# Bias of the spectral mix by a matmul that opens the accumulation, and the soft threshold as the minimum of y + lambda and relu(y - lambda), read out of PSUM

## Chip, cores and metric

One core of one Trainium2 chip runs the kernel. The metric is the device time of one execution in microseconds. Before the change it is 3775.99 us, the median of 3 runs (3766.45 to 3784.93).

## What is computed

The input x has 8 batches of 3072 rows of 256 features. Three stages follow each other:

```python
X = np.fft.rfft(x, axis=1)
Yr = Xr @ w_r - Xi @ w_i + b_r
Yi = Xr @ w_i + Xi @ w_r + b_i
lam = 0.01
Yr = np.sign(Yr) * np.maximum(np.abs(Yr) - lam, 0.0)
Yi = np.sign(Yi) * np.maximum(np.abs(Yi) - lam, 0.0)
y = np.fft.irfft(Y, n=x.shape[1], axis=1)
...
out[do_compute] = xc + gate_w * (relu(xc @ w1[e]) @ w2[e])
...
return elu(h @ w_in) @ w_out
```

The middle two lines, for the 24,576 rows of the first stage's result, are a mixture of 8 experts, of which each token takes the best one, if it takes any. The last is a dense layer with an ELU.

## The kernel before

The program has three phases, one after the other. The first does the transform along the sequence, the spectral mix and the routing of the tokens, the second the experts (a loop over tiles of 384 tokens), the third the dense layer. The change touches the first phase alone.

**The transform.** 3072 is split as 96 x 32. `forward` (L398 on) reads a batch in 8 pieces of 96 x 4 x 256 (tile `x`, for the first batch also `yv`), rounds each to float32r (`xa`), takes the rest (`xb`), multiplies with the constant `fh` and its rest `fl` on TensorE (L424, three matmuls in place of one of full precision), copies the result out of PSUM (`av`) and stores it to DRAM (`ta`). The constant `fwd` comes in 8 pieces through the tile `tr`, of which 3 live at a time; `tr` also stages the other constants, among them `w_r` and `w_i`, and later holds what the inverse transform reads.

**The middle.** `middle` takes a batch in 12 pieces p of two tiles each, and for every second batch a 13th of one tile for frequency 48: 100 pieces in all, 96 of them with two tiles. A piece is loaded (`t`), goes through the DFT of length 32 (L470, `ps<-mb,t`) and is rounded and split from PSUM (`xh` on ScalarE, `xl` on VectorE). Then comes the mix, 12 matmuls of 256 columns for each tile (L501), so 24 for a piece, into one PSUM bank `py`. Behind the mix stand three VectorE steps:

```python
nc.vector.tensor_tensor(v(y), self.tiles[py][:, :n, :], self.bias.to_broadcast([128, n, D]), op=ALU.add)
nc.vector.tensor_scalar(v(c), v(y), LAM, -LAM, op0=ALU.min, op1=ALU.max)
nc.vector.tensor_tensor(v(y), v(y), v(c), op=ALU.subtract)
```

The first (L510) adds the bias and frees the bank, the second (L517) clips to plus or minus lambda, the third (L522) takes the clipped part off. ScalarE rounds the result (`sh`), VectorE or GpSimd takes the rest (`sl`, L235), and three matmuls of 512 columns (L534, `ps<-sh,mph` and so on) start the inverse transform. The result is copied out (`cv`) and stored (`ct`).

**The inverse and the routing.** `inverse` reads `ct` in 8 pieces (`tr`), rounds and splits them (`th`, `tl`), multiplies with `inh` and `inl` (L576), turns the blocks (L589, `turn`), splits them again (`yth`, `ytl`) and computes the gate's logits (L634). `route` turns these into list positions: a chain of small VectorE steps that ends in `cnt` (L723), two small matmuls (L731, L732), `ix` (L743), and then GpSimd scatters the tokens to the experts' lists, 12 or 6 instructions for a chunk (L748). `Prep` splits the third phase's float64 weights on VectorE in the same stretch (L853 to L874).

**What sets the order.** All of the first phase is a list of steps in `Flow`. Each step has an engine (or several that can take it, with a cost for each), a due time, and the tiles that it reads and writes; of each tag, a fixed number of tiles lives at a time (7 PSUM banks `ps`, one `c`, two each of `y`, `sh`, `sl`). `Flow.order` builds the instruction order of every engine ahead of time with these costs: of the steps that could start first, the one that is due first. Roundings (`round`) go to ScalarE or VectorE, rests (`rest2`) to VectorE or GpSimd, whichever would end first by these costs. The costs are the numbers in the code, and a change in one moves steps on all engines. DMAs are issued from two queues: loads from the SyncE queue (SP), stores of `ta`, `ct` and the rows of the result from the ScalarE queue. Each queue and each engine runs in its order.

Of the kernel before, what the change touches and what calls it, by code (L numbers as in the profile page):

```python
# [11 lines left out]
F32 = mybir.dt.float32  # L12
F32R = mybir.dt.float32r
I32 = mybir.dt.int32
AF = mybir.ActivationFunctionType
ALU = mybir.AluOpType
AX = mybir.AxisListType

B, S, D = 8, 3072, 256
# [12 lines left out]
def shape_constants():  # L32
    # rows of a tile: real parts of frequencies 2 t and 2 t + 1, then imaginary parts; frequency 48 alone at the end
# [11 lines left out]
    for j in range(2):  # L45
# [11 lines left out]
    f = np.float32  # L57
    return {
# [4 lines left out]
        "tri": np.triu(np.ones((128, 128), f), 1),  # L63
    }


class Flow:
    """Steps of the engines in the order in which their inputs, buffers and engines come free.

    A step reads and writes tiles by key (tag, ...); of a tag, bufs[tag] tiles live at a time.  # L70
    Of the steps that could start, an engine takes the one that is due first.
    """
# [6 lines left out]
    def add(self, ways, due, r=(), w=(), since=0):  # L79
        """ways: (engine, cost, what to do) of each engine that can take the step."""  # L80
# [13 lines left out]
    def order(self):  # L94
        """The steps' actions in order of their start."""
# [57 lines left out]
class Phase1:  # L153
# [93 lines left out]

    def consts(self):
# [3 lines left out]
        wst = lambda: self.t(("tr", "w")).rearrange("p (h i) d -> p h (i d)", h=2)  # noqa: E731  # L252
# [3 lines left out]
        self.bias = cr.tile([128, 1, 256], F32, tag="bias", name="bias")  # L256
# [5 lines left out]
        for q in range(8):  # L262
# [6 lines left out]
            at = lambda v, s=s: v[:, s, :]  # noqa: E731  # L269
# [15 lines left out]
        def load_m():  # L285
            nc.sync.dma_start(mpf, c["mp"])
            for i, v in enumerate((self.b_r, self.b_i)):
                nc.sync.dma_start(
                    self.bias[64 * i : 64 * i + 64, 0, :], v.rearrange("(o d) -> o d", o=1).to_broadcast([64, 256])
                )  # L290

        add("DMA", 1350, -1.5, load_m, w=[("r", "mp")])
# [20 lines left out]
        trif = lambda: self.t(("tr", "tri"))[:, 0, 0:128]  # noqa: E731  # L313
        self.tri = cp.tile([128, 128], F32R, tag="tri", name="tri")
        zero = cp.tile([128, D // 128], F32, tag="zero", name="zero")
        pad = cp.tile([128, 98, 2], I32, tag="pad", name="pad")
# [5 lines left out]
        def small():  # L322
            nc.vector.memset(zero, 0.0)
            nc.vector.memset(pad[:, :, 0:1], 0)
# [68 lines left out]

    def at(self, b):
        """When the middle of batch b is due."""
        return 12 * b + (b + 1) // 2
# [943 lines left out]
```

## Time and profile before

| | |
|---|---|
| median of 3 runs | 3775.99 us (3766.45 to 3784.93) |
| span of the profiled execution, first to last instruction | 3687.1 us |
| median less the span | 88.9 us |
| first phase | about 0 to 885 us of the span |
| second phase | about 885 to 1535 us |
| third phase | about 1535 to 3687 us |
| busy share of the span | TensorE 96%, VectorE 66%, ScalarE 64%, GpSimd 18% |

The page lists the span of the profiled execution and not its own time; the time is set against the median of the runs, and the 88.9 us between the two lie around the span. The shares are means over three phases with different limits, so the first phase has to be read by itself, from the busy times of its stretches and from what its engines waited for. Line numbers are those of the kernel before. A matmul's row shows how long one takes from start to end; matmuls overlap, so what one costs in a row of them is the distance between starts.

### The profile page before, as it was taken

To read this page: it belongs to the slowest core of one execution; us is meant where nothing else is said; L and a number is where in the kernel's file an instruction comes from. 1 tells how busy PE (TensorE), PEld (TensorE's weight loads), DVE (VectorE), ACT (ScalarE), POOL (GpSimd) and SP (SyncE) were. 2 spreads that over 40 slices of the span, in tenths; PEclk is the share of its full clock that TensorE was granted. 3 is DMA by queue.
4 is the path that set the end of the run, shared out by engine and by line. 5 is a ranking of instruction groups with operands and counts; after the bars stand their busy time and mean duration, and the time that the engine had idled before them with its cause. 6 is when DMAs were issued, how large, how long until landed. Compare 5 with 4: busy or idle time off the path is not lost.

```text
span 3687.1 us, 60200 instructions
## 1 busy us (share of the span) xinstructions
PE 3546.0 (96%) x20256; PEld 3131.5 (85%) x20256; DVE 2425.7 (66%) x4475; ACT 2345.5 (64%) x4483; POOL 671.2 (18%) x742
## 2 busy tenths in 40 slices
PE   7998999996999999799999999999999999999999
PEld 7988888885999999688888888888888888888888
DVE  6988989995777777555555555555555555555555
ACT  5665656553556556466666666666666666666666
POOL 0153654445454445200000000000000000000000
PEclk8999999998999999899999999999999999999999
DMA  8876766664555555611111111111110111111100
GB/s 231 250 210 200 212 196 201 184 191 132 164 161 165 162 162 169 171 24 23 24 24 23 24 24 23 29 30 24 24 23 24 23 24 24 23 24 24 23 18 18
DMA packets 280331, 341.30 MB, mean 93 GB/s; under 512 B 129105, under 2 KB 225898, under 8 KB 280113
## 3 DMA queue, kind: packets, MB, share of 16 engines
q1 hardware_dynamic: 222240, 234.67, 23.1%
q10 hardware_dynamic: 41216, 76.56, 6.5%
q0 software_dynamic: 16656, 27.21, 2.5%
q8 instruction: 131, 2.15, 0.3%
q14 instruction: 88, 0.71, 0.1%
HBM read 214.02 MB, written 126.05 MB: 92 GB/s over the span
## 4 chain that ended last, share of the span: by engine, by line
PE 58%; DMA 0%; DVE 0%; SPq 0%; ACT 0%; issue 0%; DVEq 0%
PE ph L1198 29%; PE py L1229 19%; PE py L1232 10%; DMA x<-x 0%; SPq L1176 0%; DVE o L1239 0%; DVE xt L1185 0%; ACT xh L1187 0%; DVE xl L1188 0%; ACT o L1238 0%; DVEq L1185 0%
## 5 line engine op out<-in xcount | busy, mean ns | idle before, releaser
L1229 PE MATMUL py<-wo,gh 128*128 128x512 f32 x3072 | 1116.6, 397 | 0.0
L1198 PE MATMUL ph<-xh,wi 128*128 128x512 f32 x3072 | 1080.4, 392 | 20.2 <-ACT xh L1187 20.1
L1211 DVE SCALAR_TENSOR_TENSOR e<-m,ph 128x512 f32<-128x512 f32 x768 | 528.6, 688 | 843.1 <-ACT m L1210 843.1
L1232 PE MATMUL py<-wo,gl 128*128 128x256 f32 x3072 | 863.2, 281 | 0.0
L1209 ACT ACTIVATE m<-ph 128x512 f32<-128x512 f32 x768 | 456.6, 594 | 462.1 <-PE ph L1198 459.4
L1198 PEld LDWEIGHTS ph<-xh,wi 128*128 128x128 f32 x3072 | 577.6, 188 | 150.7 <-ACT xh L1187 21.2
L1229 PEld LDWEIGHTS py<-wo,gh 128*128 128x128 f32 x3072 | 577.3, 188 | 137.1
L1232 PEld LDWEIGHTS py<-wo,gl 128*128 128x128 f32 x3072 | 576.8, 188 | 32.4
L1198 PE MATMUL ph<-xl,wi 128*128 128x512 f32 x1536 | 603.3, 393 | 0.0
L1218 DVE TENSOR_TENSOR gl<-e,gh 128x512 fp32r<-128x512 f32 x768 | 526.4, 685 | 0.2 <-ACT gh L1217 0.2
L1210 ACT ACTIVATE m<-m 128x512 f32<-128x512 f32 x768 | 485.4, 632 | 24.6
L1217 ACT ACTIVATE gh<-e 128x512 fp32r<-128x512 f32 x768 | 472.8, 616 | 0.3 <-DVE e L1211 0.3
L1198 PEld LDWEIGHTS ph<-xl,wi 128*128 128x128 f32 x1536 | 289.8, 189 | 34.9 <-DVE xl L1188 0.9
L1053 PE MATMUL py<-w2x,hh 128*128 128x512 f32 x864 | 306.3, 395 | 0.0
L748 POOL DMA_INDIRECT lst<-pay,ix x192 | 228.4, 1190 | 118.5 <-DVE ix L743 53.8
L1056 PE MATMUL py<-w2x,hl 128*128 128x256 f32 x864 | 241.9, 280 | 0.0
L501 PE MATMUL ps<-wh,xh 128*128 128x256 f32 x784 | 228.2, 291 | 5.4 <-ACT av L228 3.6
L501 PE MATMUL ps<-wh,xl 128*128 128x256 f32 x784 | 225.2, 287 | 3.0 <-DVE xl L244 2.6
L501 PE MATMUL ps<-wl,xh 128*128 128x256 f32 x784 | 224.5, 286 | 0.0
L1042 ACT ACTIVATE hh<-ph 128x384 fp32r<-128x384 f32 x288 | 141.5, 491 | 89.1 <-ACT w2x L1017 58.1
L1040 PE MATMUL ph<-xh,w1h 128*128 128x384 f32 x576 | 193.3, 336 | 0.7 <-DVEq L1116 0.7
L1040 PE MATMUL ph<-xl,w1h 128*128 128x384 f32 x576 | 193.1, 335 | 0.0
(188 smaller groups left out, 5783.5 us busy)
## 6 DMA issues: line engine op xcount, KB each, us to landing
w1r<-in_moe_w_dram SPq DMA_DIRECT2D x37, 1024.0 KB
w2r<-in_moe_w_dram SPq DMA_DIRECT2D x37, 1024.0 KB
ta<-av ACTq DMA_DIRECT2D x64, 392.0 KB
tr<-ct SPq DMA_DIRECT2D x64, 392.0 KB
t<-ta SPq DMA_DIRECT2D x96, 256.0 KB
ct<-cv ACTq DMA_DIRECT2D x96, 256.0 KB
x<-yv ACTq DMA_DIRECT2D x64, 384.0 KB
x<-x SPq DMA_DIRECT2D x192, 128.0 KB
```

The source lines that it names most:

```text
L501: nc.tensor.matmul(o[:, t, :], a[:, 2 * t + h, at : at + 128], w[:, h, ws], start=k == 0, stop=k == 11)
L1040: nc.tensor.matmul(ph, w[:, h, fs], x[:, h, :], start=k == 0, stop=k == 5)
L1053: nc.tensor.matmul(py.rearrange("p a d -> p (a d)"), self.hh[:, f, js], self.w2x[:, f, :], start=f == 0, stop=False)
L1056: nc.tensor.matmul(py[:, 0, :], self.hl[:, f, js], self.w2x[:, f, 0:256], start=False, stop=f == nf - 1)
L1198: nc.tensor.matmul(ph, w[:, h, fs], x[:, h, :], start=k == 0, stop=k == 5)
L1209: nc.scalar.activation(m, ph, AF.Relu, scale=-1.0)
L1210: nc.scalar.activation(m, m, AF.Exp, scale=-1.0)
L1211: nc.vector.scalar_tensor_tensor(e, m, 1.0, ph, op0=ALU.subtract, op1=ALU.max)
L1217: nc.scalar.activation(gh, e, AF.Copy)
L1218: nc.vector.tensor_tensor(gl, e, gh.bitcast(F32), op=ALU.subtract)
L1229: nc.tensor.matmul(py.rearrange("p a d -> p (a d)"), gh[:, js], self.wo[:, f, :], start=f == 0, stop=False)
L1232: nc.tensor.matmul(py[:, 0, :], gl[:, js], self.wo[:, f, 0:256], start=False, stop=f == 15)
```

## The change

The bias leaves VectorE. A constant `sel` of 34 x 128 has ones in rows 0 and 32 for the first 64 output rows (real parts) and in rows 1 and 33 for the last 64 (imaginary parts). A tile `bias` of 34 x 256 holds the two bias vectors rounded to float32r in rows 0 and 1 and their rests in rows 32 and 33. One matmul of `sel` with `bias`, repeated for both tiles of a piece (512 columns), opens the accumulation of each mix; the 24 matmuls of the mix now only add, and one of them, the last, closes. The soft threshold becomes two steps: ScalarE writes c = relu(y - lambda) out of PSUM, and VectorE writes the minimum of y + lambda and c, y again out of PSUM. The loads of the two bias vectors, broadcast to 64 rows each, are replaced by a memset, a load of `sel`, four loads of one row each and the rounding; they are staged through a tile of the tag `tr`. The costs of the steps in the order's list are set anew with the steps.

```diff
+    sel = np.zeros((34, 128), f)
+    for i in range(2):
+        sel[[i, 32 + i], 64 * i : 64 * i + 64] = 1.0
...
-        self.bias = cr.tile([128, 1, 256], F32, tag="bias", name="bias")
+        self.sel, self.bias = (cr.tile([34, n], F32R, tag=t, name=t) for t, n in (("sel", 128), ("bias", 256)))
+        bsel = lambda: self.t(("tr", "b"))[:34, 1, :128]
+        braw = lambda: self.t(("tr", "b"))[:34, 0, :]
...
         def load_m():
             nc.sync.dma_start(mpf, c["mp"])
+
+        def load_b():
+            nc.sync.dma_start(bsel(), c["sel"])
             for i, v in enumerate((self.b_r, self.b_i)):
-                nc.sync.dma_start(
-                    self.bias[64 * i : 64 * i + 64, 0, :], v.rearrange("(o d) -> o d", o=1).to_broadcast([64, 256])
-                )
-
-        add("DMA", 1350, -1.5, load_m, w=[("r", "mp")])
+                for at in (i, 32 + i):
+                    nc.sync.dma_start(braw()[at : at + 1, :], v.rearrange("(o d) -> o d", o=1))
+
+        def bias_hi():
+            self.copy(self.sel, bsel())
+            self.copy(self.bias, braw())
+
+        add("DMA", 450, -1.5, load_m, w=[("r", "mp")])
+        add("DVE", 300, -3, lambda: nc.vector.memset(braw(), 0.0), w=[("tr", "b")])
+        add("DMA", 2250, -2.5, load_b, w=[("tr", "b")])
+        add("ACT", 600, -1, bias_hi, r=[("tr", "b")], w=[("r", "bhi")])
+        add(
+            "DVE", 350, -0.5, lambda: self.rest(self.bias[32:34, :], braw()[32:34, :], self.bias[32:34, :]),
+            r=[("tr", "b"), ("r", "bhi")], w=[("r", "bias")],
+        )
...
             def mix(xh=xh, xl=xl, py=py, n=n):
                 o, xh, xl = self.p(py, [128, 2, D]), self.t(xh), self.t(xl)
+                bias = self.bias.rearrange("p (o d) -> p o d", o=1).to_broadcast([34, n, D])
+                nc.tensor.matmul(o[:, :n, :], self.sel, bias, start=True, stop=False)
...
-                                    o[:, t, :], a[:, 2 * t + h, at : at + 128], w[:, h, ws], start=k == 0, stop=k == 11
+                                    o[:, t, :], a[:, 2 * t + h, at : at + 128], w[:, h, ws], start=False,
+                                    stop=k == 11 and t == n - 1,
...
-            add("PE", 2600 * f, d + 1, mix, r=[xh, xl, ("r", "wh"), ("r", "wl")], w=[py])
-
+            add("PE", 2830 * f, d + 1, mix, r=[xh, xl, ("r", "wh"), ("r", "wl"), ("r", "bias")], w=[py])
+
+            add(
+                "ACT", 480 * f, d + 1.5,
+                lambda c=c, py=py, n=n, v=v: nc.scalar.activation(
+                    v(c), self.tiles[py][:, :n, :], AF.Relu, bias=self.lam
+                ),
+                r=[py], w=[c],
+            )
             add(
                 "DVE", 600 * f, d + 1.5,
-                lambda y=y, py=py, n=n, v=v: nc.vector.tensor_tensor(
-                    v(y), self.tiles[py][:, :n, :], self.bias.to_broadcast([128, n, D]), op=ALU.add
+                lambda y=y, c=c, py=py, n=n, v=v: nc.vector.scalar_tensor_tensor(
+                    v(y), self.tiles[py][:, :n, :], LAM, v(c), op0=ALU.add, op1=ALU.min
                 ),
-                r=[py, ("r", "mp")], w=[y],
-            )
-            add(
-                "DVE", 335 * f, d + 1.5,
-                lambda y=y, c=c, v=v: nc.vector.tensor_scalar(v(c), v(y), LAM, -LAM, op0=ALU.min, op1=ALU.max),
-                r=[y], w=[c],
-            )
-            add(
-                "DVE", 600 * f, d + 1.5,
-                lambda y=y, c=c, v=v: nc.vector.tensor_tensor(v(y), v(y), v(c), op=ALU.subtract),
-                r=[c], w=[y],
+                r=[py, c], w=[y],
             )
```

Since `Flow.order` works with the new steps and costs, every engine's order moves. Of the steps that may go to either of two engines, VectorE takes 46 more roundings that ScalarE had (19 of `yth`, 9 `yv`, 7 `av`, 8 `xa`, 3 `th`) and one piece of `fh`; of the rests it takes 6 `tl` and 4 `xb` more from GpSimd and gives it 7 `sl`. TensorE has 100 matmuls more and VectorE 147 rows fewer.

**VectorE at the first pieces of the first batch's middle.** `wb`, `wa` and `wq` belong to the splitting of the third phase's weights, `inl` is a constant of the inverse. Before:

```order
L510 TENSOR_TENSOR y<-ps,bias 128x512
L244 TENSOR_TENSOR xl<-ps,xh 128x4x128
L517 TENSOR_SCALAR c<-y 128x512
L856 SCALAR_TENSOR_TENSOR wa<-bits,wa 128x512
L522 TENSOR_TENSOR y<-y,c 128x512
L510 TENSOR_TENSOR y<-ps,bias 128x512
L244 TENSOR_TENSOR inl<-tr,inh 98x384
L235 TENSOR_TENSOR sl<-y,sh 128x512
```

Now:

```order
L542 SCALAR_TENSOR_TENSOR y<-ps,c 128x512
L249 TENSOR_TENSOR xl<-ps,xh 128x4x128
L875 TENSOR_SCALAR wb<-bits 128x512
L240 TENSOR_TENSOR sl<-y,sh 128x512
L876 TENSOR_SCALAR wb<-wb 128x512
L877 TENSOR_SCALAR wa<-wb 128x512
L542 SCALAR_TENSOR_TENSOR y<-ps,c 128x512
```

Of a piece's three steps between mix and rounding one is left, and the rest `sl` follows three rows behind `y`, where it was seven rows behind the first of the three.

**ScalarE at the same place.** Before:

```order
L241 ACTIVATE xh<-xh 128x4x64
L241 ACTIVATE xl<-xl 128x4x64
L241 ACTIVATE inh<-tr 98x384
L241 ACTIVATE sh<-y 128x512
L241 ACTIVATE xh<-ps 128x4x128
```

Now:

```order
L535 ACTIVATE c<-ps,lam 128x512
L246 ACTIVATE xh<-ps 128x4x128
L246 ACTIVATE sh<-y 128x512
L246 ACTIVATE xh<-xh 128x4x64
L246 ACTIVATE xl<-xl 128x4x64
L535 ACTIVATE c<-ps,lam 128x512
```

The relu of each piece stands as one more ScalarE step ahead of the piece's rounding `sh`, with one or more steps of other pieces between them.

**The SP queue at the start.** Here the last pieces of the constant `fwd`, the bias and the mix's weights are loaded among the pieces of x. Before:

```order
L407 DMA yv<-in_x_dram 96x1024
L267 DMA tr<-in_fwd_dram 96x392 x3
L407 DMA yv<-in_x_dram 96x1024
L407 DMA x<-in_x_dram 96x1024
L275 DMA mb<-in_mb_dram 128x128
L279 DMA tr<-in_w_r_dram 128x2x256
L279 DMA tr<-in_w_i_dram 128x2x256
L286 DMA mpf<-in_mp_dram 128x128
L288 DMA bias<-in_b_r_dram 64x256
L288 DMA bias<-in_b_i_dram 64x256
L407 DMA x<-in_x_dram 96x1024 x6
```

Now:

```order
L274 DMA tr<-in_fwd_dram 96x392 x2
L429 DMA yv<-in_x_dram 96x1024
L429 DMA x<-in_x_dram 96x1024
L296 DMA tr<-in_sel_dram 34x128
L299 DMA tr<-in_b_r_dram 1x256 x2
L299 DMA tr<-in_b_i_dram 1x256 x2
L282 DMA mb<-in_mb_dram 128x128
L293 DMA mpf<-in_mp_dram 128x128
L429 DMA x<-in_x_dram 96x1024
L274 DMA tr<-in_fwd_dram 96x392
L429 DMA x<-in_x_dram 96x1024
L286 DMA tr<-in_w_r_dram 128x2x256
```

The bias takes five issues in place of two and stands ahead of the last piece of `fwd`, which now comes after the first piece of the second batch's x.

## Rows read from the trace of the kernel before

**Rows 1.** The page: span, and TensorE's busy tenths in 40 slices.
```profile
span 3687.1 us, 60200 instructions
...
PE   7998999996999999799999999999999999999999
```

**Rows 2.** Windows by stage: us; busy us (count) by engine; clock; DMA share; GB/s.
```profile
0.00:75.00 75.00, 52.31 (x308) 49.33 (x309) 43.69 (x96) 39.80 (x69) 6.92 (x19) 0.80 0.85 248
75.00:815.00 740.00, 683.32 (x5245) 649.54 (x5244) 661.26 (x1171) 451.33 (x873) 309.45 (x204) 0.97 0.69 203
815.00:885.00 70.00, 39.22 (x277) 33.98 (x275) 44.27 (x171) 26.15 (x49) 49.50 (x48) 0.79 0.55 165
...
1535.00:3687.10 2152.10, 2143.51 (x10752) 1808.54 (x10752) 1188.54 (x1920) 1453.87 (x2592) 0.00 (x0) 1.00 0.12 27
```

**Rows 3.** Windows of 100 us in the first phase, columns as in rows 2.
```profile
100.00:200.00 100.00, 96.78 (x771) 93.11 (x770) 88.58 (x141) 65.12 (x123) 13.59 (x7) 1.00 0.85 252
...
300.00:400.00 100.00, 87.62 (x627) 82.41 (x628) 84.75 (x148) 58.05 (x111) 50.11 (x34) 0.91 0.69 199
...
700.00:800.00 100.00, 97.66 (x777) 93.16 (x777) 92.71 (x181) 61.19 (x127) 39.07 (x34) 1.00 0.59 174
```

**Rows 4.** TensorE's waits, 75 to 815 us: total us, times, longest us.
```profile
PE ps L534 <- DVE sl L235: 10.9, 13, 1.8
PE ps L534 <- POOL sl L235: 9.4, 6, 2.6
PE pl L634 <- DVE ytl L244: 7.8, 4, 4.2
PE ps L731 <- DVE cnt L723: 7.6, 4, 3.2
PE ps L534 <- ACT sh L241: 6.4, 7, 1.7
PE ps L424 <- DVE xl L244: 4.0, 1, 4.0
...
PE ps L501 <- DVE xl L244: 2.6, 2, 1.6
```

**Rows 5.** VectorE's groups, first phase: busy us, mean ns, idle us before them.
```profile
L522 DVE TENSOR_TENSOR y<-y,c 128x512 f32<-128x512 f32 x96 | 66.6, 694 | 0.4
...
L510 DVE TENSOR_TENSOR y<-ps,bias 128x512 f32<-128x512 f32 x96 | 65.6, 683 | 3.8 <-PE ps L501 3.6
...
L517 DVE TENSOR_SCALAR c<-y 128x512 f32<-128x512 f32 x96 | 46.3, 482 | 0.6
```

**Rows 6.** Groups of operations like those that the change adds or moves.
```profile
L1211 DVE SCALAR_TENSOR_TENSOR e<-m,ph 128x512 f32<-128x512 f32 x768 | 528.6, 688 | 843.1 <-ACT m L1210 843.1
...
L228 ACT ACTIVATE cv<-ps 128x512 f32<-128x512 f32 x83 | 49.2, 593 | 42.0 <-PE ps L534 34.3 <-DMA ct<-cv 4.0 <-DMA bits<-in_moe_w_out_dram 1.6
...
L229 DVE COPY cv<-ps 128x512 f32<-128x512 f32 x13 | 8.9, 683 | 1.2 <-PE ps L534 1.2
...
L235 DVE TENSOR_TENSOR tl<-tr,th 98x1024 fp32r<-98x1024 f32 x45 | 58.7, 1304 | 7.1 <-ACT th L228 6.2 <-DMA bits<-in_moe_w_in_dram 0.7
```

**Rows 7.** TensorE's timeline, three matmuls of 512 columns in a row: start, us.
```profile
761.03 0.40 PE L534 MATMUL ps<-sl,mph 128*128 128x512 f32 x1
761.26 0.39 PE L534 MATMUL ps<-sh,mpl 128*128 128x512 f32 x1
761.50 0.28 PE L501 MATMUL ps<-wh,xh 128*128 128x256 f32 x1
```

**Rows 8.** TensorE's longest kind of single wait in the first 75 us.
```profile
PE ps L424 <- ACT xa L228: 8.6, 3, 6.2
```

**Rows 9.** GpSimd's timeline at the first phase's end: first and last scatter, first gather.
```profile
817.58 0.99 POOL L748 DMA_INDIRECT lst<-pay,ix  x1 [10.09 <-DVE lt L649]
...
880.44 0.98 POOL L748 DMA_INDIRECT lst<-pay,ix  x1 [0.30 <-issue]
885.11 1.04 POOL L974 DMA_INDIRECT rn<-x,pn  x1 [3.69 <-issue]
```

More of the change, by code (lines that the diff above doesn't have):

```diff
@@ L63, in shape_constants @@
         "tri": np.triu(np.ones((128, 128), f), 1),
+        "sel": sel,
     }
@@ L315, in consts @@
         zero = cp.tile([128, D // 128], F32, tag="zero", name="zero")
+        self.lam = cp.tile([128, 1], F32, tag="lam", name="lam")
         pad = cp.tile([128, 98, 2], I32, tag="pad", name="pad")
@@ L323, in small @@
             nc.vector.memset(zero, 0.0)
+            nc.vector.memset(self.lam, -LAM)
             nc.vector.memset(pad[:, :, 0:1], 0)
@@ L1277, in run, with tile_afno_moe_ffn @@
                     self.finish(a[0])
-def tile_afno_moe_ffn(tc, x, w_r, w_i, b_r, b_i, w_skip, w_gate, w1, w2, w_in, w_out, fwd, mb, mp, inv, tri, out):
+def tile_afno_moe_ffn(tc, x, w_r, w_i, b_r, b_i, w_skip, w_gate, w1, w2, w_in, w_out, fwd, mb, mp, inv, tri, sel, out):
     nc = tc.nc
@@ L1283, in tile_afno_moe_ffn @@
     lst = nc.dram_tensor("lst", (NE * CAP, 2), I32, kind="Internal").ap()
-    cst = {"fwd": fwd, "mb": mb, "mp": mp, "inv": inv, "tri": tri}
+    cst = {"fwd": fwd, "mb": mb, "mp": mp, "inv": inv, "tri": tri, "sel": sel}
     prep = Prep(tc, w_in, w_out)
```

## Prediction

> **What bounds the kernel now.** I read the page first, then the busy times by stretch, TensorE's waits, and last the groups that the change removes. In the page's slices [rows 1] TensorE stands at nine tenths almost throughout, with a dip at the start, one where the first phase ends and one where the second does. Only the first phase is touched. The third, 2152 of the 3687 us, has TensorE busy for 2143.5 us at full clock [rows 2] and takes nothing from this change; neither does the second.
>
> The first phase has three parts [rows 2]. From 0 to 75 us the pipeline fills, with the DMA engines busy at 0.85 and TensorE at 52 of 75 us. From 75 to 815 us it runs: in 740 us TensorE is busy 683.3, VectorE 661.3, ScalarE 451.3 and GpSimd 309.5. From 815 to 885 us the last batch's inverse and routing run out. So two engines are near full in the long part, and the change takes work from one and gives some to the other. The reader should see that TensorE loses twice there. It is idle for 740 - 683.3 = 56.7 us, and its mean granted clock is 0.97, so the lower level (1.2 GHz) holds in about 6% of the time and costs about 0.03 x 740 = 22 us. The stretches show that both losses go together and are not spread evenly [rows 3]: in 100 to 200 and 700 to 800 us TensorE is busy at 96.8 and 97.7% with a clock of 1.00, in 300 to 400 us at 87.6% with 0.91.
>
> What ended the idle time is in the list of waits [rows 4]. The three L534 rows, the first matmuls behind the soft threshold, make 10.9 + 9.4 + 6.4 = 26.7 us: they wait for `sl` or `sh`, the end of the chain that the change shortens. The other large ones, `ytl` 7.8, `cnt` 7.6 and `xl` 4.0 and 2.6, are VectorE steps that come late, 22.0 us together. So VectorE's load and this chain stand behind most of the 56.7 us.
>
> **VectorE's side.** Removed are three steps for each of 96 full pieces, 65.6 + 46.3 + 66.6 = 178.5 us [rows 5]. Added is one scalar-tensor-tensor of 128 x 512 with one operand in PSUM; L1211 is the same form and takes 0.688 us [rows 6], 96 x 0.688 = 66.0. The four half pieces add about -2.5 by the same proportion. Net -115 us. The order gives some of it back by moving either-engine steps to VectorE: 19 `yth` of 384 columns at no more than 0.683 = 13.0, 16 copies of 512 columns (`av`, `yv`) at 0.683 = 10.9, 11 roundings and 10 rests of 1024 columns at no more than 1.304 = 27.4, less 7 `sl` at 0.694 = 4.9 [rows 5, 6]: +46 at most. VectorE ends at 661 - 115 + 46 = 592 us.
>
> **ScalarE's side.** 96 relus out of PSUM, priced by the copy `cv` of the same shape and source at 0.593 us [rows 6]: 57 us, less what the 46 moved roundings take away. It stays below 451 + 57 = 508 of 740 us, so it has room; its cost is put at nothing, covered by its idle time. If that cover fails, a late relu holds the bank, the threshold step and the piece behind it.
> The trace has the copy of 128 x 512 out of PSUM at 0.593 us on ScalarE and at 0.683 us on VectorE [rows 6]. The Trainium skill, "ScalarE: Activation LUTs", Rules for kernel authors, says the contrary of what this edit does: relu, min and add belong on VectorE, which it gives as up to about three times faster (it names bf16). An estimate by that factor would make the 96 relus 3 x 0.683 x 96 = 197 us and fill ScalarE to some 650 us; with fp32 out of PSUM the rows decide, and the sum stays at 57.
>
> **TensorE's side.** 96 matmuls of 512 columns and 4 of 256. Starts of such matmuls in a row lie 0.23 to 0.24 us apart [rows 7]; 96 x 0.235 + 4 x 0.12 = 23 us. From below, up to 3 us may fall into the wait of L501 for `xl`, 2.6 us, since the new matmul needs no `xl` [rows 4]: 20 us. From above, a matmul that did not overlap at all would cost its 0.39 to 0.40 us: 38 us. I take 23, since all other matmuls of the phase overlap.
> The Trainium skill, "TensorE: Matmul & The Clock Gate", Back-to-back issue gap, gives about 131 ns for 512 columns in a sustained stream; that would make it 13 us and the sum 10 us better. The row's 0.235 decides.
>
> **The chain.** Between a mix and L534 there were `y`, `c`, `y`, `sh`, `sl`, so four passes through VectorE's queue and one through ScalarE's; now `c`, `y`, `sh`, `sl`, two and two. In busy time it is shorter by 0.683 + 0.482 + 0.694 - 0.593 - 0.688 = 0.58 us a piece. The bank is held longer by about one relu, 0.6 us, of 7 banks; late evacuations show in the waits as the `xl` row of L424, 4.0 us [rows 4], so from nothing to another 8 us. I take nothing, since VectorE comes to it sooner.
>
> **The start.** The SP queue gets five small issues for two, and the last piece of `fwd` stands behind them and behind a piece of x that waits for its buffer. In between TensorE has other pieces. Its longest single wait there is 6.2 us [rows 8], so I bound this by 0 and 6 us and take 2.
>
> **The end.** The last 48 scatters run on GpSimd without a gap from 817.58 to 881.4 us, and the second phase's first gather follows at 885.11 [rows 9]. This end hangs on the first of the 48, which comes when the running part is over; it shifts with it and keeps its length.
>
> **The sum.** In the running part TensorE's work at full clock is 683 - 22 = 661 us, with the bias 684. With 592 us VectorE has more slack than in either of the good stretches of [rows 3] (88.6 and 92.7% there; 592 of 712 is 83%). If the whole part ran as they do, at 96.8%, it would take 707 us; I take 96%, as the static order will leave some waits: 684 / 0.96 = 712. That is 740 - 712 = 28 us won, less 2 at the start: 26. Most of it is the return of 50 of the 79 us of idle time and low clock, paid with 23. The span goes from 3687 to 3661; with the 88.9 us around it unchanged, the time from 3776 to 3750 us.
>
> **Rivals.**
> (a) *The added matmuls hit the bound and the waits stay.* TensorE is the fullest engine, and L534 now waits behind two ScalarE passes, in a queue that also issues stores and has the relu where the order put it. Then 23 + 2 us are lost and nothing is won: 3776 + 25 = 3801. New waits of the size that the L534 rows have now would make it 3828, and with 6 us returned it is 3795. So it decides from less than 6 of the 79 us. For it speaks that every engine's order is dealt anew, and that 300 to 400 us ran badly with VectorE at only 85% [rows 3], so its load is not all; against it, that L534 and late VectorE steps are 49 of the 57 us [rows 4].
> (b) *A draw.* Between 6 and 42 us come back, and the bias matmuls eat them: 3795 to 3759. For it speaks that VectorE has idle time already, so that the order of the steps counts beside their load; against it, that the chain loses two VectorE passes.
> (c) *Nearly all of the idle time goes.* 98% gives 684 / 0.98 = 698 us and a gain of 40; all of the 79 us would give 79 - 23 - 2 = 54: 3736 to 3722. For it speaks 700 to 800 us, with 97.7% [rows 3]; against it, that 97.7% is the best stretch now and no mean.
> (d) *The bias matmul costs more than its columns*, 38 us: the forecast becomes 3765.
>
> **How the numbers follow.** About 0.5% (19 us) is what a measurement can tell from no change: 3757 and 3795. The forecast, 3740 to 3757, has 0.35, (c) 0.15, (b) together with (d) 0.34, (a) 0.16. So faster is 0.5, same 0.34, slower 0.16. The range goes from 3720, below the end of (c), to 3796, the beginning of (a), and leaves (a) out. The likeliest case's own range is 3740 to 3757.
>
> **What would show it.** Right: the new matmul's starts 0.235 us ahead of the mix's, 100 of them; VectorE about 70 us lower in the running part, which lasts some 712 us; the L534 waits well under half; the clock nearer 1.00 there; scatters still 64 us from first to last. Wrong: L534 waiting for `sh` or VectorE's threshold waiting for the relu as long as before, ScalarE's waits for the mix holding `xh` back, the first 75 us grown by more than 6, or the 300 to 700 us stretches still near 90% and 0.95.

## The result, and the profile after

The changed kernel takes 3801.55 us (median of 4 runs, 3799.51 to 3806.03); the kernel before, beside it, 3771.41 (4 runs, 3766.45 to 3784.93). The ratio is 1.0078, 95% interval 1.0058 to 1.0097: slower by 30 us, where 26 us faster was forecast. One thing is needed to read the numbers below: from one set of runs to another the kernel before itself took 3745, 3772, 3745, 3691 and 3692 us (medians), so every ratio is taken against the kernel before in the same set.

The page after: span, TensorE's busy tenths and its clock in 40 slices, against [rows 1].

```profile
span 3797.7 us, 60257 instructions
...
PE   8999989995899999979999999999999999999999
...
PEclk8999999897999999989999999999999999999999
```

The windows by stage and three of 100 us, columns as in [rows 2]:

```profile
0.00:75.00 75.00, 57.61 (x333) 52.10 (x334) 46.15 (x104) 44.37 (x78) 8.05 (x20) 0.82 0.85 246
75.00:815.00 740.00, 700.29 (x5003) 631.46 (x5003) 549.81 (x957) 451.07 (x862) 254.40 (x189) 0.95 0.66 196
...
100.00:200.00 100.00, 99.91 (x745) 90.57 (x743) 72.66 (x107) 67.57 (x128) 7.43 (x5) 1.00 0.78 234
...
300.00:400.00 100.00, 91.90 (x636) 83.03 (x634) 72.36 (x131) 56.83 (x110) 36.64 (x30) 0.91 0.66 193
...
700.00:800.00 100.00, 89.64 (x606) 79.95 (x605) 65.31 (x124) 52.75 (x105) 33.47 (x29) 0.90 0.51 150
```

In the same 740 us VectorE is busy 549.8 us against 661.3 [rows 2], but in these 740 us the change also gets less of the phase done. Over the whole first phase, up to the second phase's first gather, VectorE goes from 749.2 to 674.9 us, 74 less; the forecast had 69 less (115 less 46). Before, then after:

```profile
0.00:885.10 885.10, 774.85 (x5826) 732.85 (x5826) 749.23 (x1437) 517.28 (x989) 365.86 (x271) 0.94 0.69 204
```

```profile
0.00:951.60 951.60, 844.45 (x5926) 758.98 (x5926) 674.86 (x1290) 550.06 (x1044) 326.96 (x268) 0.92 0.64 189
```

TensorE is busier in the 740 us, 700.3 against 683.3, yet it gets through fewer matmuls, 5003 against 5245. In 100 to 200 us it is 99.91% busy at a clock of 1.00 and starts 745 matmuls; in [rows 3] it was 96.78% busy and started 771. The matmuls of the two stretches differ, so this is only a sign of a matmul that occupies TensorE for longer than its columns; the run with 128 rows, below, has the same order to hold it against. In 300 to 400 us nothing has become better: 91.90%, clock 0.91, as poor as 87.62% and 0.91 in [rows 3], although VectorE is down from 84.75 to 72.36.

TensorE's waits from 75 to 815 us (total us, times, longest us), to be held against [rows 4]:

```profile
PE ps L525 <- issue: 8.6, 12, 1.7
PE ps L611 <- issue: 4.5, 3, 1.8
...
PE ps L556 <- DVE sl L240: 0.5, 2, 0.3
```

The three rows behind the threshold, 26.7 us in [rows 4] (L534 there, L556 here), are all but gone. In their place stand rows for which the trace names no engine ("issue"), the largest ahead of L525, in the middle of a mix. VectorE and ScalarE have a new pair of waits, VectorE for the relu and the relu for the mix:

```profile
DVE y L542 <- ACT c L535: 50.6, 30, 8.4
```

```profile
ACT c L535 <- PE ps L525: 100.4, 56, 4.9
```

The first phase ends later; GpSimd's timeline has the first of the last 48 scatters, the last of them, and the second phase's first gather, against [rows 9]:

```profile
870.17 0.99 POOL L770 DMA_INDIRECT lst<-pay,ix  x1 [16.43 <-DVE lt L671]
...
944.76 0.98 POOL L770 DMA_INDIRECT lst<-pay,ix  x1 [0.30 <-issue]
951.61 1.04 POOL L996 DMA_INDIRECT rn<-x,pn  x1 [5.87 <-issue]
```

The bias matmul itself, in TensorE's timeline (start, us), among matmuls that stand 0.12 us apart:

```profile
149.84 0.28 PE L598 MATMUL ps<-tl,inh 98*96 98x256 f32 x1
149.97 0.27 PE L598 MATMUL ps<-th,inl 98*96 98x256 f32 x1
150.17 0.50 PE L517 MATMUL ps<-bias,sel 34*128 34x512 f32 x1
150.60 0.39 PE L525 MATMUL ps<-wh,xh 128*128 128x256 f32 x1
150.82 0.28 PE L525 MATMUL ps<-wl,xh 128*128 128x256 f32 x1
150.94 0.28 PE L525 MATMUL ps<-wh,xl 128*128 128x256 f32 x1
```

It starts 0.20 us after the matmul ahead of it, the mix 0.43 after it, and the mix's second matmul 0.22 after its first. Without a gap these would be 0.12, 0.235 [rows 7] and 0.12. So a piece loses 0.08 + 0.195 + 0.10 = 0.37 us beside the columns, 96 pieces 36 us.

**Theory A**: changing from 128 rows to 34 and back empties TensorE's pipeline at both edges. **Rival B**: the time is lost in the threshold's new waits. **Theory C**: the relu in ScalarE's queue eats the relief. **Theory D**, the forecast's own: VectorE's load stands behind TensorE's waits. Later came E and F: the relief is given back whatever is relieved; the static order that the planner deals decides.

### The profile page after: what moved, and what is told of

Read it like the earlier page. It is cut to its first block, busy times and chain, and to the rows that moved or that the text cites. A ratio compares the mean times of both kernels' runs of the same rounds, so it can differ in the third digit from the quotient of the medians.

```text
span 3797.7 us, 60257 instructions
## 1 busy us (share of the span) xinstructions
PE 3636.8 (96%) x20356; PEld 3158.7 (83%) x20356; DVE 2348.6 (62%) x4328; ACT 2373.5 (62%) x4538; POOL 632.8 (17%) x739
## 4 chain that ended last, share of the span: by engine, by line
PE 56%; DMA 0%; DVE 0%; SPq 0%; ACT 0%; issue 0%; DVEq 0%
PE ph L1220 28%; PE py L1251 19%; PE py L1254 10%; DMA x<-x 0%; SPq L1198 0%; DVE o L1261 0%; DVE xt L1207 0%; ACT xh L1209 0%; DVE xl L1210 0%; ACT o L1260 0%; DVEq L1207 0%
## 5 line engine op out<-in xcount | busy, mean ns | idle before, releaser
L1254 PEld LDWEIGHTS py<-wo,gl 128*128 128x128 f32 x3072 | 576.8, 188 | 32.5
L1075 PE MATMUL py<-w2x,hh 128*128 128x512 f32 x864 | 318.7, 407 | 23.6 <-DVE w2x L1040 23.6
L525 PE MATMUL ps<-wh,xh 128*128 128x256 f32 x784 | 239.2, 305 | 4.0 <-issue 3.8
L525 PE MATMUL ps<-wl,xh 128*128 128x256 f32 x784 | 227.6, 290 | 3.3 <-issue 3.3
L525 PE MATMUL ps<-wh,xl 128*128 128x256 f32 x784 | 227.3, 290 | 1.9 <-issue 1.9
L1075 PEld LDWEIGHTS py<-w2x,hh 128*128 128x128 f32 x864 | 162.0, 187 | 76.9 <-DVE w2x L1040 44.9
L770 POOL DMA_INDIRECT lst<-pay,ix x192 | 206.9, 1077 | 96.4 <-issue 52.8
L1065 DVE SCALAR_TENSOR_TENSOR hl<-ph,hh 128x384 fp32r<-128x384 f32 x288 | 159.6, 554 | 79.6 <-issue 53.1
```

Of the source, the lines that this page charges most:

```text
L525: nc.tensor.matmul(o[:, t, :], a[:, 2 * t + h, at : at + 128], w[:, h, ws], start=False, stop=k == 11 and t == n - 1,)
L770: ins = nc.gpsimd.indirect_dma_start(out=self.lst, out_offset=bass.IndirectOffsetOnAxis(ap=T(ix)[:, n : n + 1], axis=0), in_=T(pay)[:, n, ...
L1075: nc.tensor.matmul(py.rearrange("p a d -> p (a d)"), self.hh[:, f, js], self.w2x[:, f, :], start=f == 0, stop=False)
L1254: nc.tensor.matmul(py[:, 0, :], gl[:, js], self.wo[:, f, 0:256], start=False, stop=f == 15)
```

## The experiments

**First set: parts of the change** (the kernel before 3745.3 us, 28 runs).

*The kernel before once more*, unchanged.

> The kernel before, unchanged, with a profile of a new execution. In the changed kernel's execution the time is 1.8 us above the span (3799.5 and 3797.7), so the 88.9 us between the first trace's span (3687.1) and the median of before cannot lie around the span: that execution was quicker than the timed ones. If so, this profile shows a span within about 5 us of its own time, 3760 to 3785, and it tells in which phase the 80 us lie. Rival: before has some 90 us around its span, and the span is again 3680 to 3700.

Measured: 3744.3 us, 0.9995 (0.9978 to 1.0012). Its trace, span 3740.4, gives a second picture of the kernel before: first gather at 911.92, against 885.11 in [rows 9], and 678.21 us of TensorE in 75 to 815 us.

*128 rows.* The same order on every engine as the change:

```
-    sel = np.zeros((34, 128), f)
+    sel = np.zeros((128, 128), f)
...
-        self.sel, self.bias = (cr.tile([34, n], F32R, tag=t, name=t) for t, n in (("sel", 128), ("bias", 256)))
+        self.sel, self.bias = (cr.tile([128, n], F32R, tag=t, name=t) for t, n in (("sel", 128), ("bias", 256)))
```

> The bias matmul with its operands padded by zero rows from 34 to 128 partitions, all costs in the planner's list and so the order as in the changed kernel. Theory A (a matmul of 34 rows among matmuls of 96 to 128 rows empties the array before and after itself): in the changed kernel's trace the start of the bias matmul lies 0.20 us behind the last full-row start in place of 0.12, the mix's first matmul 0.43 us behind it in place of 0.235, the second 0.22 in place of 0.12, so 0.61 us a piece in place of 0.235; with 128 rows the extra 0.37 us go, about 37 us for 100 pieces: 3765 (3755 to 3772). Theory B (the relu on ScalarE and the newly dealt order cost the time): nothing changes, 3798 to 3806.

Measured: 3749.88 us, 1.0017 (1.0004 to 1.0030). More multiplications by zero, and 0.6% less time than the change (23 us, where theory A expected 37 and B nothing). In 100 to 200 us TensorE starts the same 745 matmuls as in the change and is busy 95.67 us for 99.91. Its timeline has no gap left, 0.12, 0.24 and 0.11 us:

```profile
100.00:200.00 100.00, 95.67 (x745) 90.95 (x743) 72.22 (x108) 67.11 (x128) 7.69 (x5) 1.00 0.78 238
```

```profile
148.29 0.28 PE L598 MATMUL ps<-th,inl 98*96 98x256 f32 x1
148.41 0.40 PE L517 MATMUL ps<-bias,sel 128*128 128x512 f32 x1
148.65 0.28 PE L525 MATMUL ps<-wh,xh 128*128 128x256 f32 x1
148.76 0.28 PE L525 MATMUL ps<-wl,xh 128*128 128x256 f32 x1
```

*No bias matmul*: that line is taken out and the first matmul of each half opens the sum. The order is else the change's. The bias is left out of the spectrum.

> The changed kernel without the bias matmul; the bias is left out of the result, the mix's own first matmuls open the accumulation, all costs in the planner's list stay, so the order of everything else is the changed kernel's. Theory A: the whole 0.61 us of 100 pieces go, about 60 us: 3742 (3732 to 3755). Theory B: only the 23 us of its columns go: 3779 (3773 to 3785).

Measured: 3736.12 us, 0.9976 (0.9964 to 0.9988). Against the change 1.02% or 38 us are gone, between the 60 of theory A and the 23 of B. A matmul of full rows costs 1.0017 - 0.9976 = 0.41%, 15 us, less than its 23 us of columns; and all the rest of the change together, its new order included, wins 9 us, so B, which has it lose time, falls.

*The 34-row matmul with the old threshold*, which takes clip and difference on VectorE straight from PSUM (the planner deals this one its own order):

```
-                "ACT", 480 * f, d + 1.5,
-                lambda c=c, py=py, n=n, v=v: nc.scalar.activation(
-                    v(c), self.tiles[py][:, :n, :], AF.Relu, bias=self.lam
+                "DVE", 600 * f, d + 1.5,
+                lambda c=c, py=py, n=n, v=v: nc.vector.tensor_scalar(
+                    v(c), self.tiles[py][:, :n, :], LAM, -LAM, op0=ALU.min, op1=ALU.max
...
-                lambda y=y, c=c, py=py, n=n, v=v: nc.vector.scalar_tensor_tensor(
-                    v(y), self.tiles[py][:, :n, :], LAM, v(c), op0=ALU.add, op1=ALU.min
+                lambda y=y, c=c, py=py, n=n, v=v: nc.vector.tensor_tensor(
+                    v(y), self.tiles[py][:, :n, :], v(c), op=ALU.subtract
```

> The bias matmul of 34 rows kept, the threshold on VectorE again: clip of PSUM, then PSUM less the clip, no relu on ScalarE; VectorE loses the bias addition (66 us) and has about 18 us more for the clip out of PSUM. Theory A: TensorE pays its 60 us, VectorE's relief of about 48 us wins less of the waits than the changed kernel's: 3800 to 3830. Theory B (the relu on ScalarE is at fault): the time falls below before, 3745 to 3775.

Measured: 3759.95 us, 1.0044 (1.0027 to 1.0062), between what A (1.008 and more) and B (1.001 and less) expected. VectorE does more here than in the change (614.5 us in 75 to 815 us for 549.8), and the time is no worse, though in another order.

**Second set: the drain and the load** (the kernel before 3771.71, 19 runs).

*The change again.*

> The changed kernel once more, beside the others on one chip. Theory A (the 34-row matmul drains TensorE at both of its edges) and rival B (the cost lies in the threshold's new waits) both expect 1.006 to 1.010 of the kernel before; it is the measure for the other runs of this set.

Measured: 3802.9 us, 1.0089 (1.0063 to 1.0116); the result stands.

*The bias matmul twice*: the line is repeated, the first copy with `stop=True`.

> The changed kernel with the 34-row bias matmul issued twice in succession (the second one starts the sum anew, so nothing else changes). Theory A: the cost is in the change from 128 rows to 34 and back, so a second 34-row matmul right behind the first adds only its columns, 96 x 0.235 + 4 x 0.12 = 23 us: 1.012 to 1.015 of the kernel before, and starts of the two bias matmuls 0.23 to 0.25 us apart. Rival A2: every 34-row matmul of 512 columns costs some 0.6 us of itself: 60 us more, 1.022 to 1.026. Rival A3: the second lies in the time that TensorE loses anyway: under 8 us more, 1.006 to 1.010.

Measured: 3816.56 us, 1.0121 (1.0095 to 1.0147), 0.32% or 12 us above the change beside it. The timeline:

```profile
154.80 0.28 PE L599 MATMUL ps<-th,inl 98*96 98x256 f32 x1
155.01 0.49 PE L517 MATMUL ps<-bias,sel 34*128 34x512 f32 x1
155.34 0.39 PE L518 MATMUL ps<-bias,sel 34*128 34x512 f32 x1
155.66 0.38 PE L526 MATMUL ps<-wh,xh 128*128 128x256 f32 x1
155.88 0.28 PE L526 MATMUL ps<-wl,xh 128*128 128x256 f32 x1
```

From the matmul ahead to the mix's second it is 1.08 us, against 150.82 - 149.97 = 0.85 with one: the second adds 0.23, its columns, though the two lie 0.33 apart and not the 0.23 to 0.25 expected. A price per 34-row matmul (0.6 us, 60 us in all) falls; most of the price is in the change of rows.

*128 rows and the old threshold*: the two edits above together, in the order of the 34-row kernel with the old threshold.

> Bias matmul of 128 rows, and the threshold by two VectorE steps out of PSUM (clip, then difference) in place of ScalarE's relu and one VectorE step. Against the run of 128 rows with the relu (1.0017), VectorE has some 45 us more work in the running part and ScalarE some 45 less. Theory C (the relu in ScalarE's queue is the new wait that eats the relief): 0.996 to 0.999 of the kernel before, so no worse than 1.000 and faster than with the relu. Rival D (VectorE's load sets the waits, as the forecast had it): 1.003 to 1.010, slower than with the relu.

Measured: 3763.05 us, 0.9981 (0.9963 to 0.9999). Against the same with 34 rows (1.0044, first set) again 0.6%. It is no slower than 128 rows with the relu, as C said and D did not; but the order is another, so this is a hint and no proof of C.

*No threshold*: from the kernel before, the steps of L517 and L522 are taken out (soft threshold left out).

> The kernel before without the soft threshold: clip and difference are left out, the bias stays on VectorE, and ScalarE gets nothing. So VectorE loses 46 + 67 = 113 us of work and the chain two VectorE passes, as in the forecast's best case, and no other engine pays. The routing differs, so the first phase is judged by its own end (the second phase's first gather), not by the time alone. Forecast's view (VectorE's load and this chain stand behind most of the idle time): the first phase ends 30 to 50 us sooner than in the kernel before. Theory E (the relief is given back by other waits, whatever is relieved): 5 to 20 us sooner.

Measured: 3788.64 us, 1.0048 (1.0031 to 1.0064), and the first phase ends no sooner: first gather at 939.2 us, later than the 909.8 of the kernel above in the same set (the kernel before has no trace in it; in the first set it had 911.9). Both expectations fell. 113 us less of VectorE's work, and it is slower. But the planner dealt it a new order too, which led to the next set.

**Third set: load against order** (the kernel before 3745.36, 17 runs).

*The old order, with a small threshold*: each step stands where it stood.

```
-                lambda y=y, c=c, v=v: nc.vector.tensor_scalar(v(c), v(y), LAM, -LAM, op0=ALU.min, op1=ALU.max),
+                lambda y=y, c=c, v=v: nc.vector.tensor_scalar(
+                    v(c)[:, :, 0:8], v(y)[:, :, 0:8], LAM, -LAM, op0=ALU.min, op1=ALU.max
+                ),
...
-                lambda y=y, c=c, v=v: nc.vector.tensor_tensor(v(y), v(y), v(c), op=ALU.subtract),
+                lambda y=y, c=c, v=v: nc.vector.tensor_tensor(
+                    v(y)[:, :, 0:8], v(y)[:, :, 0:8], v(c)[:, :, 0:8], op=ALU.subtract
+                ),
```

> The kernel before with its own order on every engine, but clip and difference done on 8 of each 256 columns only (the rest of the spectrum passes without a threshold; what is left out is that part of it). VectorE loses about 90 of the 113 us that these two steps take, and the chain about 0.95 us a piece, and no step changes its place. Theory F (the relief is worth what the forecast said, and the newly dealt order loses it again): 0.988 to 0.993 of the kernel before. Theory E (TensorE's waits do not hang on that load, in whatever order): 0.997 to 1.000.

Measured: 3748.75 us, 0.9998 (0.9983 to 1.0014). The two groups are down to 24.6 and 22.4 us, from 46.3 and 66.6 [rows 5], 66 us less and not the 90 expected. The windows 75 to 815 and 300 to 400 us, three of TensorE's waits, and two of the kernel before in its trace of the first set (L534 there is L538 here):

```profile
75.00:815.00 740.00, 674.51 (x5034) 633.42 (x5033) 564.39 (x1120) 433.23 (x837) 275.69 (x201) 0.95 0.68 197
...
300.00:400.00 100.00, 87.63 (x633) 82.08 (x632) 74.96 (x151) 56.05 (x106) 43.67 (x33) 0.91 0.66 188
```

```profile
PE ps L538 <- DVE sl L235: 10.9, 12, 3.4
PE ps L501 <- issue: 10.6, 23, 0.9
...
PE ps L538 <- POOL sl L235: 2.0, 3, 0.9
```

```profile
PE ps L534 <- POOL sl L235: 8.3, 6, 2.6
...
PE ps L501 <- issue: 3.8, 6, 1.0
```

In 300 to 400 us TensorE stands at 87.63% and 0.91, as in [rows 3] almost to the digit, with VectorE at 74.96 in place of 84.75. Theory D fails as an account of the time: in an unchanged order 66 us less on VectorE, on the very chain that L534 waited for, are worth nothing here. But the waits did move. Of TensorE's waits from 75 to 840 us, those for which the trace names an engine fall from 60.2 us in the kernel before (first set) to 37.7, VectorE's among them from 37.9 to 29.4; the "issue" rows rise from 6.2 to 27.0, and the sum stays, 66.4 and 64.7. So the relief did take some 22 us of waiting away, and stalls without a name stand where it was.

*The kernel before, dealt anew*: in `middle` the planner's cost of the mix is 2830 for 2600.

> The kernel before with one number changed: the planner's cost of the mix is 2830, as in the change, in place of 2600. The same steps with the same work, dealt in a somewhat other order. Theory F (the order alone moves the time by as much as the steps do): any time within 0.994 to 1.006, and off 1.000 by 0.2% or more. Rival: the order of the steps does not matter at this size, within 0.15% of the kernel before.

Measured: 3724.08 us, 0.9951 (0.9933 to 0.9969). One planner's number, no work changed, and 0.49%, some 18 us: most of the forecast's whole gain of 26. In 300 to 400 us TensorE now runs at 93.86% and 0.98 with VectorE at 92.70%, so there a busier VectorE goes with a busier TensorE:

```profile
300.00:400.00 100.00, 93.86 (x734) 88.93 (x733) 92.70 (x165) 65.28 (x127) 47.23 (x33) 0.98 0.73 217
```

*64 rows*, in the change's order.

> The changed kernel with the bias matmul padded with zeros to 64 rows. Theory A (a change between 128-row matmuls and ones of at most 64 rows drains TensorE): as with 34 rows, 1.006 to 1.010, some 0.6 us from the last matmul before a bias matmul to the second one of the mix more than usual. Rival: only the missing rows above a block of 32 make it slow; then as with 128 rows, 1.000 to 1.003.

Measured: 3773.13 us, 1.0070 (1.0050 to 1.0089). The gaps of 34 rows are there again, 0.21, 0.42 and 0.23 us:

```profile
150.91 0.27 PE L598 MATMUL ps<-th,inl 98*96 98x256 f32 x1
151.12 0.50 PE L517 MATMUL ps<-bias,sel 64*128 64x512 f32 x1
151.54 0.39 PE L525 MATMUL ps<-wh,xh 128*128 128x256 f32 x1
151.77 0.28 PE L525 MATMUL ps<-wl,xh 128*128 128x256 f32 x1
```

**Fourth and fifth set: other deals of the change** (the kernel before 3691.47, 18 runs; then 3691.59, 9 runs). Each differs from a kernel above in the planner's cost of the mix alone.

*128 rows at 3060.*

> The change with 128 rows (1.0017 before), and the planner's cost of the mix 3060 in place of 2830: same steps, other order. Theory F (the order decides by some half a per cent, whatever the steps are): off 1.0017 by 0.2% or more, within 0.994 to 1.008. Rival G (the change's steps have a time of their own, and the order matters only in the kernel before): 1.000 to 1.003.

Measured: 3655.15 us, 0.9902 (0.9885 to 0.9919), below what F (from 0.994) and G (from 1.000) expected.

*128 rows, old threshold, at 2600.*

> Bias matmul of 128 rows and the threshold by two VectorE steps (0.9981 before), with the planner's cost of the mix 2600 in place of 2830. Theory F: off 0.9981 by 0.2% or more, within 0.991 to 1.005. Rival G: 0.997 to 1.000.

Measured: 3675.49 us, 0.9955 (0.9941 to 0.9969).

*The change, 34 rows, at 3200.*

> The change itself, 34 rows, with the mix at 3200 in the planner in place of 2830, about what mix and drain take on the chip. Theory F with theory A: the drain's 23 us stay, the order moves the rest: 1.002 to 1.012, off 1.0085 by 0.2% or more. Rival G: 1.006 to 1.010. A time under 1.000 would say that the order outweighs the drain.

Measured: 3678.13 us, 0.9964 (0.9952 to 0.9975), below both expectations (from 1.002 and from 1.006): the change itself, faster than the kernel before.

*The kernel before at 3060.*

> The kernel before with the mix at 3060 in the planner in place of 2600 (with 2830 it was 0.9951). Theory F: another time again, within 0.993 to 1.006, with no rule in the number. Rival H (the order is better the dearer the planner thinks the mix): 0.995 or less.

Measured: 3687.15 us, 0.9989 (0.9978 to 0.9999). A smaller step than with 2830, so no direction in the number, and H falls as far as two sets can be compared.

*128 rows at 3060, again; the same order with 34 rows; 128 rows at 3200.*

> The run of 128 rows with the mix at 3060 in the planner, once more beside the next ones (it was 0.9902 there): 0.988 to 0.993, if the order is worth what it seemed to be.

> The same order with the change's own 34-row matmul. Theory A (the drain is a price of its own, whatever the order): 0.5 to 0.8% slower than the 128 rows beside it, as in the first order (1.0078 against 1.0017). Rival: the drain falls into waits of a better order, less than 0.3% between the two.

> 128 rows in the order of the run with the mix at 3200 (with 34 rows it was 0.9964). Theory A: 0.5 to 0.8% below that, 0.988 to 0.992. Rival as in the run with 34 rows at 3060: 0.993 to 0.997.

Measured: 3657.32 us, 0.9899 (0.9883 to 0.9914); 3674.27 us, 0.9947 (0.9933 to 0.9960); 3660.98 us, 0.9909 (0.9891 to 0.9926). The 34 rows cost 0.48% here, 17 us between two kernels of one set and one order, just under the 0.5 expected, and 0.9964 - 0.9909 = 0.55% at 3200. The windows 75 to 815 us of both at 3060, first 128 rows, then 34:

```profile
75.00:815.00 740.00, 707.55 (x5493) 673.98 (x5492) 607.25 (x1106) 496.29 (x947) 280.54 (x208) 0.98 0.72 214
```

```profile
75.00:815.00 740.00, 723.43 (x5410) 658.66 (x5410) 599.83 (x1068) 490.40 (x934) 262.45 (x198) 0.99 0.71 210
```

With 34 rows TensorE is 16 us busier and starts 83 matmuls fewer. Nearly half of the 36 us of gaps thus comes out of its idle time (32.5 to 16.6 us); the rest, some 20, is about the 17 us that the kernel loses.

The 128-row form at 3060 is the fastest of all and beats both kernels: by 1.0% the one before, measured twice, and by 0.5% the change's own rows in the same order.

## Why the prediction was wrong

**The sum, step by step.** Forecast against the kernel before: 49 us back from shorter chain and less VectorE work, less the start (28 + 23 - 2), and 23 us for the bias matmuls; together -26. Measured by the first set and the result: -9 (no bias matmul, 0.9976), +15 (a 128-row one, 1.0017), and for the 34 rows 1.0078 - 1.0017 = 0.61%, about 23. Together +29, against 30 measured. Two terms failed.

**The bias matmul** was priced at 23 us, "since all other matmuls of the phase overlap", with a bound of 38. It costs 15 + 23 = 38 us in this order, the whole upper bound. It does not overlap its neighbours as they overlap each other, because TensorE goes from 128 rows to 34 and back. Shown by the gaps (34 and 64 rows have them, 128 has none), by the doubled matmul, and by four pairs of one order each, 34 against 128 rows: 0.61% (0.72% with the second run of the change), 0.63%, 0.55% and 0.48%. Only the last pair lies within one set; it gives 17 us, so the 23 are the less certain figure. The step that failed is the choice of row: [rows 7] are matmuls of 128 rows, and no row of that trace has one of 64 or fewer beside one of 128. The 98-row ones of L598 follow one another at 0.12 us and go over into 128 rows without a gap (148.29 to 148.41 above). The Trainium skill, "TensorEngine Tiling (Array Packing)", Key Properties, has the rule that was missing: "Changing tiling mode (not just tile) drains the TensorE"; its Tiling Modes list row tilings of 64 and of 32 rows. The traces agree in that 34 and 64 rows have the gaps and 98 and 128 have none, at 0.37 us for a pair of changes. The page gives no price and does not say that a matmul of 34 rows runs in such a mode.

**The return of 50 of the 79 us** was the larger miss, 40 us of 56: 9 us came. What was said about VectorE's side held: 74 us less over the first phase for 69 forecast, the new step at 686 ns for 688. The relu takes 685 ns for 593, for which ScalarE, busy 451 of the 740 us, has room. The L534 waits went, as forecast. The step that failed is the one from these waits to time. The forecast took the waits that the chain and VectorE end as idle time that comes back, and the clock with it. In the old order, with the threshold's two steps at 47 us for 113, the waits with a named engine shrank by 22 us and the time stayed (0.9998), with 21 us more of nameless stalls in their place. Counted as the forecast counts, idle time and clock together, TensorE loses 62 + 30 = 92 us from 75 to 815 us in the first set's kernel before (clock 0.96), and 45 + 37 = 82 with 128 rows (busy 695.2 us, clock 0.95): some 10 of the 50 came, to within the 7 us that a hundredth of the clock is worth. What starts the stalls, and so why the relief was not paid out, stays open. Rival (a), given 0.16, came true. That its price of 3801 was met is luck, since the split is another: the matmul dearer, and 9 us returned. It had the sign in hand: "300 to 400 us ran badly with VectorE at only 85% [rows 3], so its load is not all". That stretch ran no better with VectorE at 75 and at 72%, and better with VectorE at 93% in another order.

**The order** is what the forecast left out of its range. It wrote "the static order will leave some waits" and put 96% on it. Dealing the same steps anew moves the kernel before by 0.49% (0.9951) and by 0.11% (0.9989). The changed steps, at 3060 and 3200, are faster than the kernel before, by 0.5 and 0.4% with 34 rows. So the result's sign belongs to this deal or its conditions and not to the steps alone. What stays open: the deals at 3060 and 3200 ran in the two sets in which the kernel before took 3691 us, and the change's own deal was not run in such a set. How much of the step from 1.0017 to 0.9899 is the order, and how much those conditions (last section), is not separated. The first and the fifth set ran on one chip, with the kernel before at 3745 and 3692 us, so the conditions are not the chip alone. The forecast's return may have come there: by the count above 128 rows at 3060 lose 32 + 15 = 47 us, the kernel before at 3060 in the same set 57 + 30 = 87, so 40 of the 50 came back, in traces without a single "issue" row.

**The base.** "88.9 us around it" was a misreading: in every later run time and span differ by 2 us. So the profiled execution must have been quicker by some 87 us than the times printed beside it, a picture of the sets at 3691. Set against that base, 3687 + 2 - 26 = 3663 us, the forecast is near what the best deals took there (3657 with 128 rows, 3674 with 34). As long as the open point is open, that is a coincidence and no success.

**Smaller points.** The start: 57.6 us of TensorE in 75 against 52.3 [rows 2], no growth. The last 48 scatters take 944.76 - 870.17 = 74.6 us from first to last, against 62.9 in [rows 9]; but the kernel before itself takes 906.73 - 833.30 = 73.4 in the first set, so this goes with the set and not with the change. Relu and hand-over: what VectorE's 50.6 us of waiting for the relu cost is not separated. With the old threshold the time was 0.3 to 0.4% lower, with 34 rows and with 128, each time in another order and set, and C stays a hint.

## What to carry to other kernels

A matmul of few rows between full ones is not priced by its columns: pad the contraction to the rows of its neighbours and it may become cheaper, as it did here from 34 and from 64 rows to 128. Before an engine's load is blamed for another's lost time, halve that load with every step left in its place; this needs two lines and would have put the forecast's return in doubt. Look then at the time as well as at the waits, since waits can shrink and the time stay. Where a planner deals the order, the same steps dealt two or three ways give the scatter that any change must exceed, and a change is fairly judged by its best deal against the best deal of the kernel before.

## What the runs showed of the hardware

Not expected were stalls of several engines at once. They are the "issue" rows above: TensorE stands in the middle of a mix, and the trace names no engine that ends its wait. One of them in the trace of the change:

```profile
546.35 0.35 PE L525 MATMUL ps<-wh,xh 128*128 128x256 f32 x1
547.04 0.37 PE L525 MATMUL ps<-wl,xh 128*128 128x256 f32 x1 [0.34 <-issue]
547.25 0.28 PE L525 MATMUL ps<-wh,xl 128*128 128x256 f32 x1
549.15 0.28 PE L525 MATMUL ps<-wh,xh 128*128 128x256 f32 x1 [1.62 <-issue]
...
553.41 0.37 PE L525 MATMUL ps<-wl,xh 128*128 128x256 f32 x1 [1.72 <-issue]
```

The windows of 10 us around it show VectorE and ScalarE idle with it, the DMA engines at 0.30 for 0.68, and the clock fall behind it:

```profile
535.00:545.00 10.00, 10.00 (x81) 9.34 (x80) 5.60 (x11) 4.79 (x11) 6.92 (x8) 1.00 0.68 207
545.00:555.00 10.00, 4.67 (x23) 3.80 (x23) 2.31 (x4) 1.24 (x3) 5.51 (x6) 0.84 0.30 83
555.00:565.00 10.00, 10.00 (x68) 9.32 (x68) 9.42 (x14) 8.45 (x16) 4.85 (x2) 0.82 0.74 211
```

TensorE loses 5 us and then pays again at a lower clock, 0.84 and 0.82 on the mean. GpSimd alone goes on, with a run of 12 scatters:

```profile
536.93 0.99 POOL L770 DMA_INDIRECT lst<-pay,ix  x1 [1.25 <-DVE ix L765]
...
551.05 0.98 POOL L770 DMA_INDIRECT lst<-pay,ix  x1 [0.30 <-issue]
```

Nearly all stalls of TensorE, VectorE and ScalarE over 0.75 us in this trace ("issue" or "remote" in the rows) lie in such runs of scatters, which come some 50 us apart, or within 4 us behind one. TensorE's "issue" rows from 75 to 840 us sum to 28.7 us in the change (22.9 when it ran again), 20.9 with 128 rows, 26.6 without the bias matmul, 27.0 with the small threshold, 30.4 without the threshold, 12.5 and 20.5 with the old threshold and 34 or 128 rows, but 6.2 and 5.9 in the kernel before and its new deal in the two sets at 3745: the forms with less VectorE work have more. In all seven kernels profiled in the two sets at 3691 us, and in the trace shown ahead of the prediction, that sum is 0, with the same runs of scatters. One thing limits these sums: the traces at 3691 hold 37,360 to 37,595 semaphore events, the others 29,660 to 30,227, so in those a wait can stand as "issue" only because the event that ended it was not recorded. The missing events lie in the first two phases, and so does the time between the sets: in the traces of the kernel before at 3687 and at 3740 us the first phase takes 885.1 and 911.9 us, the second, from its first gather to its last scatter, 636.1 and 661.2, and the rest, in which GpSimd has nothing to do [rows 2], 2165.9 and 2167.3. What starts the stalls, and whether they are what takes the relief back, no run shows.
